# First layer's input products of ten d_ff tiles as blocks of seven products for eight, in passes of batch pairs

## The chip, the cores and the metric

One core of one Trainium2 chip runs the whole program. The metric is device time in microseconds, the median of several runs. Weights arrive as float64 words and are decoded on the chip; every product is made of three fp32r matmuls (high by high, high by low, low by high).

## The reference

```python
x = attention(rmsnorm(q), rmsnorm(k), v)     # 4 batches, 12 heads, 448 rows, 64 wide
x = x.transpose(0, 2, 1, 3).reshape(1792, 768)
h = x @ w_in                                 # first layer, d_ff 2048: 16 tiles of 128
x = np.maximum(h, 0.0) ** 2 @ w_out
g, val = x @ w_gate, x @ w_val               # second layer, d_ff 1536: 12 tiles of 128
out = (g * sigmoid(g) * val) @ w_out2
```

## The kernel before, in words

Everything is kept transposed: a tile is 128 features by 448 rows of one batch, six such tiles are one batch of x. A product of one d_ff tile with one batch is 6 x 3 = 18 matmuls of 128x128 by 128x448 (`in_product`, `mm3`, L370), and so is that tile's share of the output.

**Attention** comes first. Between its matmuls a low-ranked thread (`fillers`, L1056) runs the first layer's d_ff tiles 0 to 5 for batches 0, 1 and 2 (`h_a`, `ya`), and at the end the first three products of batch 3 (`h_lead`, `lead`).

**First layer, rest.** `products` (L1205) walks over `sweeps`: batch 3 with tiles 0 to 10, then the other batches with tiles 6 to 10 and 11 to 15. For each tile: input product `h`, its square on ScalarE and VectorE (`squares`, L405 to L411), and the output product `y` two tiles later. Six PSUM banks collect a sweep's outputs. At its end VectorE adds the partial sum of earlier sweeps, loaded from HBM (`partial_sums`, `written`, L1274), and SyncE's queue stores it. The weights of tiles 6 to 15 are decoded as they come (`load_weights`), x is loaded and split into high and low halves per sweep (`load_x`).

**Second layer.** Gate and value products are taken by Strassen's scheme in Winograd's form, seven block products for eight, for pairs of batches: the operands are halves of the weights (a11, a12, a21, a22 and the sums s1 to s4) and halves of the two batches' x (b11, b21, b22 and the sums t1 to t4). Of each the plain form is stored in HBM, loaded again into a staging tile, and split from there into its final slot (`split_part`, L1452; `load_pair`, L1574). `unit` (L1633) takes the seven products of 9 matmuls each; VectorE adds them up out of PSUM (`plus`, L1677). A pass is three units of one pair of batches, then its twelve output tiles (`outputs`, `summed_out`), each of which VectorE adds to the partial sum loaded from HBM (L1804).

**Order.** The order of every engine's instructions is fixed when the program is built: threads yield jobs with a cost for each engine, and a planner (`dispatch`, `simulate`) gives each engine the best-ranked job that is ready by its own clock. It counts DMAs at 300 bytes per ns (`DMA_RATE`). On the chip the engines follow those lists and wait on semaphores.

Of the kernel before, what the change touches and what calls it, by code (L numbers as in the profile page):

```python
# [9 lines left out]
F32 = mybir.dt.float32  # L10
# [9 lines left out]
KD = DM // 128  # L20
# [5 lines left out]
M1 = 11  # L26
# [20 lines left out]
RAWS2 = 1  # L47
IO_TILES = 7
W2_SLOTS = 16
X_SLOTS = 12  # L50
P_SLOTS = 3
PAIRS = ((2, 0), (1, 3))
GROUP = 3
PARTIALS = 4
SPARES = 2
DEC_AHEAD = 2
PAIR_AHEAD = 3
LEND_RAWS = 0
LEND_TEMPS = 0
SUMS_AHEAD = 4  # L60
SUMS = 4
X_LOADS = 4
OLD_SECOND = 0
BEHIND = 2
X_AT = 3
X_FLIGHT = 3
# [23 lines left out]
PARTS = ("a11", "s2", "a12", "s1", "s4", "s3", "a22", "o0", "o1")  # L90
# [3 lines left out]
def attention_two_ffn_kernel(  # L94
# [27 lines left out]
    x2_d = [[dram.tile([128, S], F32, name=f"x2d{b}_{j}") for j in range(KD)] for b in range(B)]  # L122
    y1_d = [[dram.tile([128, S], F32, name=f"y1d{b}_{j}") for j in range(KD)] for b in range(B)]
    y2_d = [[dram.tile([128, S], F32, name=f"y2d{b}_{j}") for j in range(KD)] for b in range(B)]
    pre_d = [{n: dram.tile([128, WC], F32, name=f"{n}_d{f}") for n in PARTS} for f in range(FF2)]
    t_d = [{n: [dram.tile([128, S], F32, name=f"{n}_d{p}_{k}") for k in range(3)] for n in ("t1", "t2", "t3", "t4")} for p in range(2)]
# [87 lines left out]
    def ported(job, e):  # L214
        return e == "G" or e == "V" and "W" in job[1][0]
# [7 lines left out]
    def dispatch(e):  # L223
# [24 lines left out]
        if e == "S":  # L248
# [51 lines left out]
    wt, placed, free, seen, after = {}, {}, [], set(), []  # L300

    def load_weights(items):
# [7 lines left out]
        def chunk(key, place, c, raw_at):  # L310
# [31 lines left out]
            if c == 0:  # L342
                yield lambda: place or free
                pool, hi_tag, lo_tag = placed[key] = place or free.pop(0)
# [15 lines left out]
        for key, place, rank in items:  # L360
            if not place and after:
                yield lambda: free
                place = free.pop(0)
# [727 lines left out]
    M1B, F1C = range(G1, M1), range(M1, FF1)  # L1091
# [3 lines left out]
    sweeps += [(1, LAST - 1, range(G1, FF1), M1B, y1_d[LAST - 1], x2_d[LAST - 1])]  # L1095
    sweeps += [(1, b, F1C, (), y1_d[b], x2_d[b]) for b in range(LAST - 1)]
    sweeps += [(1, LAST, F1C, F1C, y1_d[LAST], x2_d[LAST])]
    outs = [[out[bass.ts(j, 128), bass.ts(b, S)] for j in range(KD)] for b in range(B)]
    POST = 10000
    when, steps = {}, 0  # L1100
    for layer, b, fs, *_ in sweeps:
        for f in fs:
            for key in (("in", f), ("out", f)):
                when.setdefault(key, POST + steps)
            steps += 1
# [11 lines left out]

    items = [(("in", f), place(4 * f), DEC_FIRST + DEC_STEP * f) for f in range(G1)]
    items += [(("out", f), place(4 * f + 2), OUT_FIRST + OUT_STEP * f) for f in range(G1)]
    later = [(w, f) for f in range(G1, FF1) for w in ("in", "out")]  # L1120
    items += [(key, None, when[key] - W_AHEAD) for key in later]
# [18 lines left out]
    spawn(load_weights(items), 0)  # L1140
    spawn(fillers(), 1e6, FILL)
# [4 lines left out]
    after.append(0)  # L1146
    att.close()
    xp2 = ctx.enter_context(tc.tile_pool(name="xp2", bufs=1, side="right", reuse_waits="tile"))
    mid = ExitStack()
    w2 = mid.enter_context(tc.tile_pool(name="w2", bufs=1, side="right", reuse_waits="tile"))  # L1150
    w3 = mid.enter_context(tc.tile_pool(name="w3", bufs=1, side="right", reuse_waits="tile"))
    raws += [(w3, f"raw{2 + i}") for i in range(RAWS2)]
    was += [(w3, "wa2")]
    wts += [(w3, "wt2")]
    for i in range(W2_SLOTS // 2):
        free.append((w2, f"w{2 * i}", f"w{2 * i + 1}"))
    simulate(lambda: filled and local[FILL] == 0)


    fill.close()  # L1160
    ranked.append(0)
    io = ctx.enter_context(tc.tile_pool(name="io", bufs=1, reuse_waits="tile"))
    io_free = [(io, f"io{i}") for i in range(IO_TILES)]
    ps_y = ctx.enter_context(tc.tile_pool(name="ps_y", bufs=1, space=PSUM, reuse_waits="tile"))

    def x_tiles(n, second, ts):
        def tile_of(j):
            pool = xp2 if second and j < 4 else xp
            ts[j] = pool.tile([128, 2, S], F32R, tag=f"x{j + 2 if second and j >= 4 else j}", name=f"x_{n}_{j}")
            return ts[j]  # L1170

        return tile_of

    def load_x(src, n, tiles, done, rank):

        def part(j, where):
            raw = tile_at(where, [128, S], F32, f"xr_{n}_{j}")
            yield from dma(lambda e: e.dma_start(out=raw, in_=src[j]), 128 * S * 4)
            t = tiles(j)
            yield {"A": 467, "W": 300}, lambda e: copy(e, t[:, 0, :], raw)  # L1180
            yield {"W": 535, "G": 1106}, lambda e: e.tensor_tensor(
                out=t[:, 1, :], in0=raw, in1=as_f32(t[:, 0, :]), op=ALU.subtract
            )
            io_free.append(where)
            done.append(j)

        for j in range(KD):
            yield lambda: io_free and j - len(done) < X_FLIGHT
            spawn(part(j, io_free.pop(0)), rank)

    w_free, x_free, retired = [], [], []

    def release(key):
        del wt[key]
        slot = placed.pop(key)
        if len(seen) < len(items):
            free.append(slot)
        elif slot[0] is w1:
            w_free.extend((w1, tag) for tag in slot[1:])
        else:  # L1200
            retired.append(slot)

    finished = []

    def products():  # L1205
        behind = []
        ys = {}
        xs = x1[LAST]
        k = POST
        for i, (layer, b, fs, last_use, partial, dst) in enumerate(sweeps):  # L1210
            n = f"{layer}_{i}"
            done = None
            for f in fs:
                if f == fs[X_AT if len(fs) > 6 else 1] and i + 1 < len(sweeps):
                    nxt, done = {}, []
                    spawn(load_x(x1_d[sweeps[i + 1][1]], n, x_tiles(n, i % 2 == 0, nxt), done, k), k)
                name = f"{n}_{f}"
                if i == 0 and f < 3:
                    release(("in", f))
                else:  # L1220
                    yield lambda: ("in", f) in wt
                    ps, where = yield from h_tile(f"h_{name}")
                    yield from in_product(ps, wt["in", f], xs)
                    spawn(squares(ps, where, name), k - 0)
                    if f in last_use:
                        release(("in", f))
                while len(behind) >= BEHIND:
                    yield from behind.pop(0)
                sums = {} if partial and f == fs[-1] else None
                if sums is not None:  # L1230
                    spawn(partial_sums(partial, n, sums, k - SUMS_AHEAD), k - SUMS_AHEAD)
                behind.append(out_of(name, n, f, f == fs[0], f == fs[-1], f in last_use, ys, sums, dst, k))
                k += 1
            if done is not None:
                yield lambda: len(done) == KD
                xs = nxt
            if i == len(sweeps) - 2:
                x_free.extend([(xp2, f"x{j}") for j in range(4)] + [(xp, "x6"), (xp, "x7")])
            if i == len(sweeps) - PAIR_AHEAD:
                spawn(load_first_pair(0), k)  # L1240
        x_free.extend((xp, f"x{j}") for j in range(3))
        s_free.extend((xp, f"x{j}") for j in range(3, 6))
        for gen in behind:
            yield from gen
        spawn(spares(), k - W_AHEAD)
        if not OLD_SECOND:
            spawn(pair_sums(1 - passes[0][0], k), k)
        yield from second_layer(k)
        finished.append(0)

    def spares():
        for _ in range(SPARES):
            yield lambda: io_free
            ea_free.append(io_free.pop(0))

    def partial_sums(src, n, sums, rank):

        def part(j, at):
            y = tile_at(at, [128, S], F32, f"yp_{n}_{j}")
# [663 lines left out]
```

## Time and profile before

| | before |
|---|---|
| median of 3 runs | 1231.98 us (1229.92 to 1233.0) |
| the profiled execution | 1228.38 us |
| its span, first to last instruction | 1226.6 us |
| TensorE matmuls | 6426, busy 1205.8 us |
| VectorE busy | 870.6 us |
| ScalarE busy | 630.8 us |
| GpSimd busy | 164.4 us |
| moved by DMA | 238.98 MB |

The span is what the views measure; the execution takes 1.8 us more around it, and the median run 3.6 us more than the profiled one. PE is TensorE, DVE VectorE, ACT ScalarE, POOL GpSimd, SP SyncE. Matmuls overlap in the records, so their pace is read from the length of a piece of the chain over its count, not from the mean of one. The attention's stage ends at 409.67 us, the first layer's at 738.05 us.

### The profile page before, as it was taken

Reading aid. Unit: us, or ns where it says so; the run is one execution under the profiler, and the core shown is the slowest. Engines: PE = TensorE matmul, PEld = TensorE weight load, DVE = VectorE, ACT = ScalarE, POOL = GpSimd, SP = SyncE. Lnnn points to the kernel's source line nnn. Section 1 sums busy time; section 2 is a strip of 40 time slices with the busy share of each in tenths; the row PEclk is TensorE's granted clock in tenths of the full one; section 3 lists DMA queues with packets and bytes.
Section 4 is the critical chain, followed back from the end, with each engine's and each line's share of the span. In section 5 each row is a group of like instructions: output and inputs, shape, how many; then the busy total and the mean of one; then the engine's idle time right before and its main releaser. Section 6 shows DMA issues by size and latency. Waiting matters only on the chain.

```text
span 1226.6 us, 19513 instructions
## 1 busy us (share of the span) xinstructions
PE 1205.8 (98%) x6426; PEld 1032.5 (84%) x6426; DVE 870.6 (71%) x1795; ACT 630.8 (51%) x1381; POOL 164.4 (13%) x280
## 2 busy tenths in 40 slices
PE   8989999999999999999999999999999999999998
PEld 5656667777777899999999999999999999999998
DVE  8999985665543899767665877876678676855564
ACT  6999877766765666333332443564334233422320
POOL 5454464244311000000000000000000000000000
PEclk9999999999999999999999999999999999999999
DMA  7576665334212666878576888876578756752634
GB/s 225 169 206 187 189 186 164 97 127 145 84 41 74 205 195 209 290 248 287 177 261 208 278 264 270 270 242 214 180 237 264 246 185 201 242 183 70 211 120 142
DMA packets 146934, 238.98 MB, mean 195 GB/s; under 512 B 23105, under 2 KB 126418, under 8 KB 146834
## 3 DMA queue, kind: packets, MB, share of 16 engines
q1 hardware_dynamic: 146834, 237.75, 61.0%
q8 instruction: 50, 0.82, 0.3%
q14 instruction: 50, 0.41, 0.1%
HBM read 169.51 MB, written 68.17 MB: 194 GB/s over the span
## 4 chain that ended last, share of the span: by engine, by line
PE 86%; DVE 6%; ACT 4%; DMA 3%; issue 1%; SPq 0%; ACTq 0%; DVEq 0%
PE y L370 28%; PE p L370 23%; PE h L370 13%; PE ya L370 5%; PE o L937 4%; PE h_a L370 4%; PE sc L766 4%; PE pt L897 3%; ACT ring L808 1%; DVE sc L794 1%; ACT turned_p L258 1%; PE pt L892 1%; PE pt L895 1%; PE h_lead L370 1%; DMA raw_out<-in_w_out_dram 1%
## 5 line engine op out<-in xcount | busy, mean ns | idle before, releaser
L370 PE MATMUL y<-s,o_split 128*128 128x448 f32 x864 | 176.7, 365 | 0.0
L370 PEld LDWEIGHTS y<-s,o_split 128*128 128x128 f32 x864 | 162.2, 188 | 13.2 <-DVE s L1321 0.4
L370 PE MATMUL y<-s,hi_out 128*128 128x448 f32 x552 | 157.2, 366 | 1.6 <-DVE r L407 1.6
L370 PE MATMUL h<-x,hi_in 128*128 128x448 f32 x516 | 147.3, 367 | 0.0
L370 PE MATMUL p<-t,s_split 128*128 128x448 f32 x648 | 144.5, 367 | 0.0
L370 PEld LDWEIGHTS p<-t,s_split 128*128 128x128 f32 x648 | 121.8, 188 | 11.1
L808 ACT ACTIVATE ring<-sc,m,rms 128x448 f32<-128x448 f32 x168 | 123.9, 744 | 12.6 <-DVE m L795 4.6
L1677 DVE TENSOR_TENSOR u<-p,u 128x448 f32<-128x448 f32 x144 | 88.3, 621 | 37.5 <-PE p L370 36.1
L370 PEld LDWEIGHTS y<-s,hi_out 128*128 128x128 f32 x552 | 103.5, 188 | 10.5 <-DVE r L407 2.0
L794 DVE TENSOR_REDUCE sc<-sc 128x2 f32<-128x896 f32 (+1 forms) x96 | 93.8, 977 | 16.2 <-PE sc L766 14.8
L370 PEld LDWEIGHTS h<-x,hi_in 128*128 128x128 f32 x516 | 96.9, 188 | 8.4
L370 PE MATMUL y<-s,lo_out 128*128 128x448 f32 x276 | 100.7, 365 | 0.0
L258 ACT COPY turned_p<-pt 128x384 f32<-128x384 f32 (+2 forms) x167 | 88.4, 540 | 23.4 <-PE pt L897 22.6
L370 PE MATMUL p<-b,a_split 128*128 128x448 f32 x432 | 96.2, 367 | 0.0
L370 PE MATMUL h<-x,lo_in 128*128 128x448 f32 x258 | 94.4, 366 | 0.0
L370 PEld LDWEIGHTS p<-b,a_split 128*128 128x128 f32 x432 | 81.1, 188 | 7.1
L937 PE MATMUL o<-turned_p,v 128*64 128x448 f32 x384 | 79.5, 546 | 0.6 <-DVE turned_p L260 0.5
L897 PE MATMUL pt<-ident,ring 128*128 128x128 f32 x432 | 70.7, 274 | 2.8 <-ACT ring L808 2.3
L1804 DVE TENSOR_TENSOR yp<-y,yp 128x448 f32<-128x448 f32 x72 | 43.9, 623 | 38.3 <-PE y L370 21.4
L370 PE MATMUL h_a<-x,hi_in 128*128 128x448 f32 x216 | 67.8, 381 | 0.0
L370 PE MATMUL ya<-sa,hi_out 128*128 128x448 f32 x216 | 67.3, 385 | 0.0
L405 ACT ACTIVATE r<-h 128x448 f32<-128x448 f32 x43 | 23.3, 542 | 81.2 <-PE h L370 81.1
(174 smaller groups left out, 2249.1 us busy)
## 6 DMA issues: line engine op xcount, KB each, us to landing
yp<-y2d SPq DMA_DIRECT2D x72, 224.0 KB
raw_in<-in_w_in_dram SPq DMA_DIRECT2D x32, 384.0 KB
raw_out<-in_w_out_dram SPq DMA_DIRECT2D x32, 384.0 KB
kq<-in_kq_p_dram SPq DMA_DIRECT2D x23, 480.0 KB
t_plain<-t_d SPq DMA_DIRECT2D x48, 224.0 KB
y2d<-yp SPq DMA_DIRECT2D x48, 224.0 KB
raw_a<-in_w_val_dram SPq DMA_DIRECT2D x24, 384.0 KB
raw_a<-in_w_gate_dram SPq DMA_DIRECT2D x24, 384.0 KB
```

Of the source, the lines that this page charges most:

```text
L258: e.copy(out, src)
L370: return {"P": 203}, lambda e: e.matmul(ps, lhsT=w, rhs=x, start=first, stop=last), 0
L405: yield {"A": 424}, lambda e: e.activation(out=r, in_=ps, func=ACTF.Relu)
L766: e.matmul(parts[t][:, :S], lhsT=q[a][d, bass.ts(i % 4, 128)], rhs=k[c][d], start=(p == 0), stop=(p == len(passes) - 1),)
L794: e.tensor_reduce(out=top, in_=sc, axis=AX.X, op=ALU.max, negate=True)
L808: yield {"A": 704}, lambda e: e.activation(out=slot(i), in_=parts[t][:, :S], func=ACTF.Exp, bias=m[:, t:t + 1], scale=rq[:, i:i + 1], accu ...
L892: e.transpose(pieces[:, :, j], p[:, bass.ts(j, 128)] if j < 3 else ends, ident)
L895: e.transpose(ps[:, :128], ends, ident)
L897: e.transpose(ps[:, bass.ts(j + (i > 3), 128)], p[:, bass.ts(j, 128)], ident)
L937: e.matmul(o[64 * h:64 * h + 64], lhsT=v[:, 4 * h + j], rhs=turned_p[:, 4 * h + j if j < 3 else 3], start=(j == 0), stop=(j == 3),)
L1677: return {"V": 535}, lambda e: e.tensor_tensor(out=out, in0=ps, in1=b, op=ALU.add)
L1804: yield {"V": 535}, lambda e: e.tensor_tensor(out=y, in0=ps, in1=y, op=ALU.add)
```

## The change

Tiles 0 to 5 stay as they were. Tiles 6 to 15 become five units of two d_ff tiles: a unit's weights form a 2x2 block matrix (two tiles by two halves of the model dimension), two batches' x the other, and the second layer's `unit` now serves both layers. The first layer becomes six passes: units 0 and 1 for batch pair 0 (batches 0, 1), then for pair 1 (batches 2, 3); unit 2 for pair 1, then pair 0; units 3 and 4 for pair 0, then pair 1. A pass ends with twelve output tiles, each a chain over its units' tiles.

Four more things move with it. Weights of the five units are decoded, summed and stored during attention (`decode_ahead`). Operands are loaded straight into their final slot and split in place (`split_in_place`), with no staging tile; 21 x slots hold one pair's operands. Partial sums of all passes but a pair's last are added into HBM by an accumulating DMA that GpSimd issues, where VectorE added them before. And the last first-layer outputs are handed from SBUF to the sums of the second layer's operands (`handed`).

```diff
+GROUPS1 = ((0, 1), (2,), (3, 4))
...
-    sweeps = [(1, LAST, range(M1), range(G1), None, y1_d[LAST])]
-    sweeps += [(1, b, M1B, (), y1_d[b], y1_d[b]) for b in range(LAST - 1)]
...
+    for layer, groups in ((1, GROUPS1), (2, GROUPS2)):
+        p = 0
+        for us in groups:
+            passes += [(layer, p, us), (layer, 1 - p, us)]
+            p = 1 - p
...
+        f = G1 + 2 * u
+        return [(f"a{r + 1}{c + 1}", w_in[f + r], c) for r in range(2) for c in range(2)], [
...
+    spawn(decode_ahead(), POST)
...
+    def split_in_place(t, src, c):
+
+        plain = as_f32(t[:, 1])
+        yield from dma(lambda e: e.dma_start(out=plain, in_=src), 4 * c * 128)
+        yield from halves_of(t, plain, c)
...
+        for p, a, x, then in (
+            ("p1", "a11", "b11", first_0), ("p6", "s2", "t2", sum_2), ("p2", "a12", "b21", first_0_ends),
+            ("p5", "s1", "t1", sum_4), ("p3", "s4", "b22", first_1), ("p7", "s3", "t3", second_1),
+            ("p4", "a22", "t4", second_0),
+        ):
...
+    def squared(t, at, name):
+
+        yield {"A": 467}, lambda e: e.activation(out=t, in_=t, func=ACTF.Relu)
+        yield lambda: s_free
+        s_at = s_free.pop(0)
+        s = tile_at(s_at, [128, 2, S], F32R, "s_%d_%d_%d_%d" % name)
+        yield {"A": 467}, lambda e: e.activation(out=s[:, 0], in_=t, func=ACTF.Square)
+        yield {"W": 535, "G": 1106}, lambda e: e.tensor_tensor(out=t, in0=t, in1=t, op=ALU.mult)
+        yield {"W": 535, "G": 1106}, lambda e: e.tensor_tensor(
+            out=s[:, 1], in0=t, in1=as_f32(s[:, 0]), op=ALU.subtract
+        )
...
-        if sums is not None:
+        if whole(n):
             yield lambda: (j, h) in sums
...
+            dst = y_of[layer][b][j]
+            yield lambda: (layer, b, j) in y_count
+            yield {"G": POOL_DMA}, lambda e: e.dma_start(out=dst, in_=y, accum_op=ALU.add), 2 * 128 * S * 4, POOL_LATER, True
```

**TensorE, where the first layer's tiles 6 and on begin.** Before, in the sweep of batch 3 (y are outputs, h input products of tile 10, x a k tile's halves):

```order
L370 MATMUL y_1_0_0_5486<-s_1_0_7_5891,hi_out7_5463 128x448 x2
L370 MATMUL y_1_0_0_5486<-s_1_0_7_5891,lo_out7_5464 128x448
L370 MATMUL y_1_0_1_5491<-s_1_0_7_5891,hi_out7_5463 128x448 x2
L370 MATMUL y_1_0_1_5491<-s_1_0_7_5891,lo_out7_5464 128x448
L370 MATMUL h_1_0_10_6094<-x1_18_4511,hi_in10_5758 128x448 x2
L370 MATMUL h_1_0_10_6094<-x1_18_4511,lo_in10_5759 128x448
L370 MATMUL h_1_0_10_6094<-x1_19_4676,hi_in10_5758 128x448 x2
```

And now, behind the outputs of tile 5 (p1 and p6 are block products of pass 0, unit 0):

```order
L370 MATMUL y_1_5903<-s_1_0_5_6121,hi_out5_2679 128x448 x2
L370 MATMUL y_1_5903<-s_1_0_5_6121,lo_out5_2680 128x448
L370 MATMUL p1_0_0_6228<-b11_0_0_5726,a11_1_0_split_5856 128x448 x3
L370 MATMUL p1_0_0_6228<-b11_0_1_5829,a11_1_0_split_5856 128x448 x3
L370 MATMUL p1_0_0_6228<-b11_0_2_5879,a11_1_0_split_5856 128x448 x3
L370 MATMUL p6_0_0_6250<-t2_0_0_5773,s2_1_0_split_5857 128x448 x3
L370 MATMUL p6_0_0_6250<-t2_0_1_5929,s2_1_0_split_5857 128x448 x3
```

An 18-matmul product per tile and batch has become a 9-matmul product, seven of them for two tiles and two batches: 630 in place of 720.

**SyncE's queue, where pass 1 gets its x operands.** Before there was no such load in the first layer; in the second they read (a staging tile, written ahead of the split):

```order
L1586 DMA b11_5_2_plain_11544<-x2d1_2_89 128x448
L1586 DMA t2_5_0_plain_11558<-t2_d1_0_276 128x448
L1586 DMA t2_5_1_plain_11582<-t2_d1_1_277 128x448
L1586 DMA t2_5_2_plain_11599<-t2_d1_2_278 128x448
L1586 DMA b21_5_0_plain_11631<-x2d1_3_90 128x448
```

And now (t2_d and the like are sums stored to HBM; t2_1_2 is the tile of pass 1, into its own slot):

```order
L1321 DMA t3_1_1_6484<-t3_d1_1_1_311 128x448
L1350 DMA t2_d1_1_2_309<-b22_1_1_2_6504 128x448
L1350 DMA t4_d1_1_2_315<-b21_1_1_2_6521 128x448
L1321 DMA t4_1_0_6498<-t4_d1_1_0_313 128x448
L1321 DMA t4_1_1_6522<-t4_d1_1_1_314 128x448
L1321 DMA t1_1_2_6590<-t1_d1_1_2_306 128x448
L1321 DMA t3_1_2_6609<-t3_d1_1_2_312 128x448
L1321 DMA t2_1_2_6628<-t2_d1_1_2_309 128x448
L1321 DMA t4_1_2_6635<-t4_d1_1_2_315 128x448
```

The last sums go out to HBM and come back by the same queue, as the last loads of the pass.

**GpSimd's queue, at the end of pass 0** (yw are output tiles, y1d the partial sums in HBM; there was nothing at this place before):

```order
L1774 DMA y1d1_4_91<-yw_0_4_1_6712 128x448
L1774 DMA y1d0_4_85<-yw_0_4_0_6731 128x448
L1774 DMA y1d1_5_92<-yw_0_5_1_6751 128x448
L1774 DMA y1d0_5_86<-yw_0_5_0_6770 128x448
L1138 TENSOR_TENSOR o2_1_2_split_6896<-o2_1_2_split_6896 128x384
L1138 TENSOR_TENSOR o1_1_2_split_6917<-o1_1_2_split_6917 128x384
```

Twelve accumulating DMAs now stand in GpSimd's list at the end of a pass, with operand splits of the next unit behind them.

## Rows read from the trace of the kernel before

**Rows 1.** The page: busy time by engine, and the chain that ended last.

```profile
PE 1205.8 (98%) x6426; PEld 1032.5 (84%) x6426; DVE 870.6 (71%) x1795; ACT 630.8 (51%) x1381; POOL 164.4 (13%) x280
...
PE 86%; DVE 6%; ACT 4%; DMA 3%; issue 1%; SPq 0%; ACTq 0%; DVEq 0%
```

**Rows 2.** Stretches: length; busy of PE, PEld, DVE, ACT, POOL; clock, DMA share, GB/s.

```profile
180.00:240.00 60.00, 59.45 (x359) 44.53 (x356) 36.27 (x77) 40.77 (x102) 24.41 (x44) 1.00 0.42 132
240.00:300.00 60.00, 60.00 (x364) 44.51 (x364) 35.61 (x80) 40.59 (x101) 23.86 (x43) 1.00 0.43 135
300.00:360.00 60.00, 60.00 (x366) 46.32 (x363) 32.60 (x72) 43.40 (x107) 16.64 (x16) 1.00 0.25 74
420.00:480.00 60.00, 60.00 (x297) 55.30 (x296) 59.94 (x137) 38.78 (x81) 0.00 (x0) 1.00 0.66 208
553.00:581.00 28.00, 28.00 (x139) 25.65 (x138) 20.36 (x42) 9.03 (x18) 0.00 (x0) 1.00 0.85 284
...
443.00:737.80 294.80, 294.80 (x1448) 271.60 (x1447) 219.01 (x449) 123.83 (x245) 4.45 (x4) 1.00 0.74 244
```

**Rows 3.** PE's timeline where attention ends: start, length, what, [idle before].

```profile
409.67 0.57 PE L370 MATMUL y<-s,hi_out 128*128 128x448 f32 x2
410.08 0.37 PE L370 MATMUL y<-s,lo_out 128*128 128x448 f32 x1
412.04 0.47 PE L370 MATMUL y<-s,hi_out 128*128 128x448 f32 x1 [1.59 <-DVE r L407]
```

**Rows 4.** All waits of PE from 400 us to the end.

```profile
PE y L370 <- DVE r L407: 1.6, 1, 1.6
```

**Rows 5.** The chain that ended last: start, length, what.

```profile
455.56 3.68 PE y L370 x18
...
657.60 3.69 PE h L370 x18
...
738.05 11.09 PE p L370 x54
...
859.55 38.71 PE p L370 x189
898.26 21.89 PE y L370 x108
```

**Rows 6.** DVE's timeline in the first layer: start, length, what.

```profile
430.02 0.57 DVE L338 SCALAR_TENSOR_TENSOR wt_out<-wa_out,wt_out 128x384 int32<-128x384 int32 x1
430.50 0.57 DVE L354 TENSOR_TENSOR lo_in<-wt_in,hi_in 128x384 fp32r<-128x384 f32 x1
430.96 0.64 DVE L1181 TENSOR_TENSOR x<-xr,x 128x448 fp32r<-128x448 f32 x1
431.50 0.57 DVE L354 TENSOR_TENSOR lo_out<-wt_out,hi_out 128x384 fp32r<-128x384 f32 x1
431.97 0.38 DVE L331 TENSOR_SCALAR wt_in<-raw_in 128x384 int32<-128x384 uint32 x1
```

**Rows 7.** Groups by line and shape: busy us, mean ns | idle before, releasers.

```profile
L1810 ACT COPY yw<-y 128x448 f32<-128x448 f32 x24 | 12.6, 536 | 13.0 <-PE y L370 10.9 <-DMA a_d<-a 1.3 <-DVE t L1321 0.2
...
L1363 DVE TENSOR_SCALAR a<-raw_a 128x384 int32<-128x384 uint32 x48 | 16.7, 355 | 11.2 <-DMA raw_a<-in_w_gate_dram 8.0 <-DMA raw_a<-in_w_val_dram 3.3
...
L983 POOL TENSOR_TENSOR x<-ox,x 128x448 fp32r<-128x448 f32 x24 | 27.6, 1151 | 70.9 <-ACT x L258 58.9 <-DMA v<-in_v_p_dram 5.9 <-DVE kq L704 2.7
```

**Rows 8.** The chain again: its two longest DMA pieces, issue to landing.

```profile
765.17 4.95 DMA b_plain<-x2d
...
774.37 5.15 DMA raw_a<-in_w_gate_dram
```

**Rows 9.** DMA from 500 to 700 us, in 40 slices of 5 us.

```profile
DMA  6899699469797996867454286978816639989968
GB/s 236 261 342 323 214 318 311 181 147 308 282 320 265 285 360 238 281 179 237 166 171 106 98 268 199 364 292 284 256 68 206 241 130 269 317 236 341 369 210 265
```

More of the change, by code (lines that the diff above doesn't have):

```diff
@@ L25 @@
 G1 = 6
-M1 = 11
 EPS_RMS = 1e-6
@@ L1157, in attention_two_ffn_kernel @@
[L1157 to L1189, printed above, removed]
@@ L1193, in release @@
+    operand, pair_x, summed_x = {}, {}, set()
     def release(key):
         del wt[key]
[L1195 to L1229, printed above, removed]
-                if sums is not None:
[L1231 to L1259, printed above, removed]
-            yield from dma(lambda e: e.dma_start(out=y, in_=src[j]), 128 * S * 4)
-            sums[j] = y, at
-        for m, j in enumerate(OUT_ORDER):
-            yield lambda: io_free and m < sums.get("used", 0) + SUMS
-            spawn(part(j, io_free.pop(0)), rank)
@@ new lines, in attention_two_ffn_kernel, with products @@
+    simulate(lambda: filled and local[FILL] == 0)
+    fill.close()
+    ranked.append(0)
+    given_back.append(0)
+    for at in [at for at in io_free if at in loaned]:
+        io_free.remove(at)
+        x_free.append(at)
+    io = ctx.enter_context(tc.tile_pool(name="io", bufs=1, reuse_waits="tile"))
+    io_free += [(io, f"io{i + 1}") for i in range(IO_TILES)]
+    ps_y = ctx.enter_context(tc.tile_pool(name="ps_y", bufs=1, space=PSUM, reuse_waits="tile"))
+    finished = []
+    def products():
+        k = POST
+        xs = x1[LAST]
+        behind, ys = [], {}
+        for f in range(G1):
+            name = f"1_0_{f}"
+            if f < 3:
+                release(("in", f))
+            else:
+                ps, where = yield from h_tile(f"h_{name}")
+                yield from in_product(ps, wt["in", f], xs)
+                spawn(squares(ps, where, name), k - 2)
+                release(("in", f))
+            while len(behind) >= BEHIND:
+                yield from behind.pop(0)
+            behind.append(first_out(name, f, ys, k))
+            k += 1
+        for j in range(6):
+            s_free.append((xp, f"x{j}"))
+        for gen in behind:
+            yield from gen
+        io_free.extend(ea_free)
+        yield from all_passes()
+        finished.append(0)
@@ new lines, in first_out @@
+    def first_out(name, f, ys, k):
+        yield lambda: ("out", f) in wt and name in ready
+        w = wt["out", f]
+        s, where = ready.pop(name)
+        for j in OUT_ORDER:
+            if f == 0:
+                ys[j] = ps_y.tile([128, S], F32, tag=f"y{j}", name=f"y_{j}")
+            yield from mm3(ys[j], w[0], w[1], bass.ts(j, 128), s[:, 0, :], s[:, 1, :], f == 0, f == G1 - 1)
+            if f == G1 - 1:
+                spawn(first_written(ys[j], j), k - 2)
+        s_free.append(where)
+        release(("out", f))
@@ new lines, in first_written @@
+    def first_written(ps, j):
+        yield settle["P"]
+        yield lambda: io_free
+        at = io_free.pop(0)
+        y = tile_at(at, [128, S], F32, f"ys_{j}")
+        yield {"A": 424}, lambda e: e.copy(y, ps)
+        h_free.append((ps_y, f"y{j}"))
+        yield from dma(lambda e: e.dma_start(out=y1_d[LAST][j], in_=y), 128 * S * 4)
+        y_count[1, LAST, j] = 1
+        io_back(at)
+    y_of = {1: y1_d, 2: y2_d}
+    y_count = {(1, b, j): 1 for b in range(LAST) for j in range(KD)}
@@ L1622, in second_layer, with s_free_w @@
                         spawn(partials(n, p, sums, k), k)
-                yield from unit(n, f, x_of, last_x and f == fs[-1], last_w, k)
+                yield from unit(n, (layer, u), x_of, last_x and u == us[-1], last_w, k)
                 k += 2
-            yield from outputs(n, p, fs, sums if p in summed_before else None, last_w, k)
-            summed_before.add(p)
+            yield from outputs(n, sums, last_w, k)
+    ENDS_1 = 2 * len(GROUPS1)
+    def s_free_w():
+        for _ in range(S_TO_W):
+            spawn(one_s_to_w(), POST)
@@ L1792, in outputs @@
+            yield from chain(j, h, deep[-1:] if m < ahead else deep)
+            spawn(summed_out(n, j, h, ys[j, h], sums), k)
+            if m == last_use[j // 3] and drop_w:
+                for u, r in deep:
+                    w_free.append(operand.pop(((layer, u), f"o{2 * r + j // 3}"))[1])
+        for u, r in deep:
             for h in range(2):
-                s_free.append(ready.pop((n, f, h))[1])
-    def summed_out(n, p, j, h, bank, sums):
+                s_free.append(ready.pop((n, u, r, h))[1])
@@ L1796, in summed_out @@
+    def summed_out(n, j, h, bank, sums):
         ps, where = bank
+        layer, p, _ = passes[n]
         b = PAIRS[p][h]
-        last = all(q != p for q, _ in passes[n + 1:])
-        dst = outs[b][j] if last else y2_d[b][j]
         yield settle["P"]
-        if sums is not None:
+        if whole(n):
             yield lambda: (j, h) in sums
```

754 lines of the change are left out of this document (344 added, 410 removed).

## The prediction

> **What bounds the kernel now.** I read the page first, then the stretches, then TensorE's own timeline and waits. The page shows TensorE busy for 1205.8 us of a span of 1226.6, and its work makes 86% of the chain that ended last [rows 1]; VectorE stands at 71%, ScalarE at 51%. The stretches say the same of the stage that changes: from 443 to 737.8 us TensorE is busy without a gap at a granted clock of 1.00, with VectorE at 219 of 294.8 us and DMA at 0.74 [rows 2]. From 400 us to the end TensorE waits once, 1.59 us at 412 us, for VectorE's square of a tile that is needed at once [rows 3, 4]. So a matmul taken out of this stage shortens the program by its whole length, as long as what feeds TensorE keeps up with a shorter stage.
>
> **The change part by part.**
>
> *Matmuls removed.* The pace is read from pieces of the chain [rows 5]: 18 outputs in 3.68 us, 18 input products in 3.69, 189 block products in 38.71 (0.2048 each), 108 outputs in 21.89 (0.2027). The first layer's stage runs from 409.67 [rows 3] to 738.05 [rows 5]. It holds 774 input-product matmuls (54 of tiles 3 to 5, 720 of tiles 6 to 15) and 828 output matmuls: (328.38 - 1.59) / 1602 = 0.204 us. The change takes seven products of 9 for what were eight, so 720 become 10 x 63 = 630; outputs stay 828, attention's own matmuls and fillers too. 90 x 0.204 = **-18.4 us**, all on the path.
>
> *Pace of what is left.* Blocks and long output chains take 0.2027 to 0.2048 us where they stand now, the stage's mean is 0.204. If the 720 outputs of the passes, now chains over up to four tiles in one bank, ran at 0.2027 for 0.2043, that is -1.2; if not, 0. The block products give nothing. I take -0.3.
>
> *Decoding moved into attention.* Five units' weights are read, decoded, summed and stored there: 139 more VectorE rows before the first first-layer square, 40 raw loads, 40 loads back and the stores between. By the rows of decoding (0.27 to 0.57 us [rows 6]) that is some 57 us of VectorE work. In 180 to 360 us VectorE is busy 36.3, 35.6 and 32.6 of each 60 us and DMA moves 132, 135 and 74 GB/s while TensorE is full [rows 2]: 75 us free on VectorE alone, so I cost it at nothing. Without that cover it would cost up to 57 us; the same work is taken off 420 to 480 us, where VectorE was busy 59.94 of 60 us [rows 2].
>
> *More sums.* Each unit needs seven additions out of PSUM in place of ScalarE's and VectorE's squares straight from it, 70 in all, against 48 partial-sum additions that go; ScalarE gets 96 copies of outputs at 0.54 us [rows 7]. A short pass (one unit, 27.5 us of TensorE) asks VectorE for some 15 rows of the unit (8.0 us), 18 x splits (9.6) and 8 weight splits (3.8), 21.4 us. ScalarE and VectorE are covered by TensorE: nothing. In the stretch 420 to 480 a VectorE busy to 59.94 us still held nobody up [rows 2, 4], so near-full is no stall.
>
> *Start of the first unit.* Before p1 TensorE has 54 input and 108 output matmuls left, 33 us from 409.7. VectorE's list shows 67 rows up to the last operand that unit needs first, about 0.5 us each [rows 6], so 33 us from about 402; the sum operands p5 to p4 follow with some 15 us in hand. Nothing.
>
> *Split in place.* A slot can be loaded only after TensorE's last read of it. The shortest time from freeing to need is pass 2 to 3: 54 block and 72 output matmuls, 25.7 us; elsewhere 33 to 42. One landing in a busy stretch is 4.95 to 5.15 us [rows 8], the cast and the split half a microsecond each [rows 6]: 6.2 us. Hidden.
>
> *Handover of passes.* Here the lists are tight in one place at least. For pass 1 the t2 sum of the third k tile is stored and read back as the last loads on SyncE's queue, then split on VectorE directly ahead of the sum of p6, and cast on ScalarE behind the last output of pass 0. Such a wait isn't in the trace; the nearest row is the 1.59 us at 412, a tile needed at once [rows 3, 4], and one more landing is 5.15 [rows 8]. Bounds 0 to 5.15; I take **+1.6**, because the queue's order leaves the tile behind by a step, not by a whole transfer.
>
> *Accumulating DMAs.* 96 in all: 48 in the first four passes, where they replace a load, a VectorE addition and a store, and 48 in the second layer's. No row of before shows one on GpSimd or its rate. By bytes, SyncE's queue now asks for 76.3 MB from attention's end to the last first-layer load, and 48 accumulates of 0.229 MB count c times: 87, 98, 109 MB for c of 1, 2, 3. Five-microsecond slices reach 369 GB/s where the stage's mean is 244 [rows 9, 2], so 328 us could hold 121 MB; a stretch at 284 GB/s had DMA at 0.85 and TensorE still full [rows 2]. Taken at nothing for c of 2; they begin to cost, on the mean, at c of 3.9. For the issue itself the nearest GpSimd row is a tensor operation of 1.15 us [rows 7]: twelve take 13.8 us of a 27.5 us pass. Nothing. In the second layer the same DMAs and splits in place have passes of three units (189 block and 108 output matmuls, 38.71 + 21.89 us [rows 5]), over twice the time: nothing there either. The Trainium skill's page "SBUF — State Buffer" ("A bandwidth-pool intuition that's wrong") speaks against this: a DMA from GpSimd that takes about 620 ns alone took about 3100 ns beside a VectorE copy, since its descriptors wait for a shared port. By that figure twelve would need 37 us of a 27.5 us pass and the sum would be 19 us higher, an estimate from that page that no run here bears out yet; VectorE's rows are short here (0.355 us [rows 7] to 0.64 [rows 6]).
>
> *Sum.* -18.4 - 0.3 + 1.6 = -17.1. The profiled execution took 1228.38, so 1211.3; the median of the runs shown is 3.6 higher, 1231.98, so 1214.9: **1215 us**.
>
> **The rivals.** A measurement of this kernel can tell about 0.3% from no change, 3.7 us: "same" is 1228.3 to 1235.7.
>
> *1. DMA becomes the bound at the handovers.* From pass 0 to 1 the list has 33 loads and stores (7.6 MB) and 12 accumulates in 54 + 144 + 15 matmuls, 43.3 us, which hold 16.0 MB at 369 GB/s [rows 9]: enough up to c of 3.05. From 2 to 3 it is 5.8 MB and 12 accumulates in 38.4 us: again 3.05. At c of 4, or as much lost to small transfers, each is 7.1 us late, 14.2 in all: 1229. For it: the stage's mean was already 0.74 busy, the slices swing between 68 and 369 [rows 9], and the planner counts 300 bytes per ns with no landing delay. Against: TensorE never waited at 0.85 [rows 2, 4]. The Trainium skill's "DMA: Bandwidth & Descriptors" (Issuing engines are not separate DMA queues) holds that GpSimd's transfers share the same engines, so that its queue brings no bandwidth of its own; the runs here show nothing on that yet. 1222 to 1229, chance 0.17 (0.11 of it faster, 0.06 same).
>
> *2. GpSimd's queue becomes the bound, and the kernel slower.* Each output tile lies in a buffer until its accumulating DMA is through, the buffers stop ScalarE's copies, these the PSUM banks, these TensorE. With T us for each DMA on GpSimd, passes 2 and 3 (27.5 us, twelve each) decide from T = 2.3; the loss is 2 x (12 T - 27.5). Slower by over 0.3% needs T above 3.15; T = 3.5 gives 1215 + 29 = 1244. For it: nothing in the trace prices such a DMA, and split operands stand behind them in GpSimd's list. Against: the nearest GpSimd row, 1.15 us [rows 7]. Chance 0.11 (0.10 slower). The page named above would give T = 3.1 and 1234, just inside "same" (0.01).
>
> **How the numbers follow.** The forecast has 0.72. Its own range is 1210 (no handover wait, the full -1.2 of pace, and some 2 us for the draw of a median whose runs lie 3.1 apart) to 1219 (a wait of 5.15). With rival 1 at its upper end the range becomes 1210 to 1229; outside lie rival 2 and what of the forecast falls below. Faster 0.72 + 0.11 = 0.83; same 0.06 + 0.01 = 0.07; slower 0.10.
>
> **What would show it.** In the profile after, TensorE's count should be 6336, the first layer should end at about 721 us with the second unchanged in length, and attention should end within 2 us of 409.67. Waits of TensorE, if any, should stand at p6 of pass 1 and sum to under 5 us. GpSimd's DMAs should lie under 2.3 us apart, no slice of the first layer should stay at 369 GB/s for 15 us, and VectorE should gain load in 180 to 360 and lose it in 420 to 480. Rival 1 would show waits at each first product of a pass, released by DMA; rival 2 waits of outputs behind ScalarE's copies, those behind GpSimd. I am wrong in the main if attention's end moves or if waits exceed 7 us; wrong in the pace if 189 block products of the first layer take other than 38.7 us.

## The result, and the profile after

The change made the kernel slower: 1242.59 us (1240.6 to 1244.87, four runs) against 1230.95 for the kernel before in the same session, a ratio of 1.0093 with a 95% interval of 1.0070 to 1.0117. The forecast was 1215, the range 1210 to 1229, and "slower" had a chance of 0.10.

| | before | after |
|---|---|---|
| median | 1230.95 us | 1242.59 us |
| span of the profiled execution | 1226.6 | 1240.7 |
| first outputs behind attention's last wait | 412.04 [rows 3] | 431.89 (+19.85) |
| from there to the second layer's first product | 326.01 (to 738.05 [rows 5]) | 314.57 (-11.44) |
| from there to the end of the span | 488.55 | 494.24 (+5.7) |

The three differences add up to the 14.1 us between the two spans. 412.04 stands behind three outputs that had already run and 431.89 ahead of them, so like for like attention moved by 0.6 us more, and the first layer gained 0.6 us more. The first layer did get shorter. What ate its gain stands ahead of it, in attention, and to a smaller part behind it.

The page of the changed kernel, busy time and the chain that ended last, against [rows 1]:

```profile
PE 1199.1 (97%) x6336; PEld 1017.5 (82%) x6336; DVE 919.5 (74%) x1877; ACT 705.0 (57%) x1550; POOL 289.9 (23%) x411
...
PE 69%; DVE 10%; DMA 9%; ACT 7%; issue 3%; SPq 1%; POOL 0%; DVEq 0%; ACTq 0%; POOLq 0%
```

The 90 matmuls are gone (6426 to 6336), but TensorE's share of the chain fell from 86% to 69%, and VectorE, ScalarE and DMA share what it lost: the end is now set in part by chains that run through them. The stretches say where, with the columns of [rows 2]:

```profile
180.00:240.00 60.00, 54.85 (x327) 39.18 (x324) 42.54 (x93) 38.36 (x94) 23.39 (x39) 1.00 0.68 209
240.00:300.00 60.00, 58.25 (x347) 43.21 (x347) 48.89 (x107) 47.23 (x115) 24.45 (x38) 1.00 0.71 211
300.00:360.00 60.00, 55.49 (x322) 40.71 (x322) 43.26 (x99) 42.92 (x106) 20.00 (x29) 0.97 0.63 189
```

TensorE was full here before; now it lacks 1.8 to 5.2 us in each 60, while VectorE never passes 49 and ScalarE 48 of 60. So no engine is the bound by its load: something is late. Two views of waits in attention name it. TensorE's two longest, the second of them the one that ends attention (without it, its waits from 180 us on come to 12.0 us):

```profile
PE pt L897 <- DVE ox L959: 4.6, 3, 2.7
PE y L370 <- DVE r L407: 4.4, 1, 4.4
```

and ScalarE's for the raw words of weights, which the change decodes here (total, times, longest):

```profile
ACT raw_o L1163 <- DMA raw_o<-in_w_out_dram: 22.4, 11, 6.4
...
ACT raw_a L1163 <- DMA raw_a<-in_w_in_dram: 12.0, 7, 3.9
```

ScalarE stood still for 34 us in these two groups, waiting for words, with attention's rows behind it in its fixed list (in the kernel before, its waits for words of weights came to 7.5 us in the same stretch). One such place, on all engines' timelines:

```profile
338.58 0.98 SPq L1160 DMA_DIRECT2D raw_a<-in_w_in_dram  x2
...
343.46 0.58 ACT L1163 ACTIVATE raw_a<-raw_a 128x384 f32<-128x384 f32 x1 [3.90 <-DMA raw_a<-in_w_in_dram]
...
343.46 0.36 DVE L1169 TENSOR_SCALAR raw_a<-raw_a 128x384 int32<-128x384 uint32 x1 [2.93 <-DMA raw_a<-in_w_in_dram]
...
346.68 0.61 DVE L959 TENSOR_TENSOR ox<-o,zb 128x448 f32<-128x448 f32 x1
...
347.35 0.90 PE L897 MATMUL pt<-ident,ring 128*128 128x128 f32 x3 [2.67 <-DVE ox L959]
```

Read it from the top: two loads of raw words are issued at 338.6; ScalarE and VectorE both reach the rows that read the first of them and stand until 343.46, 4.9 us after its issue. With nothing ahead of it the planner counts 1100 + 393216 / 300 + 900 ns, 3.3 us, for such a load. Behind the decoding stands `ox`, the quotient that attention's next transpose waits for, and TensorE idles 2.67 us. Then something follows that the waits don't show; stretches with their granted clock:

```profile
347.30:350.50 3.20, 3.15 (x10) 2.90 (x11) 2.55 (x5) 3.17 (x9) 3.17 (x3) 0.50 0.72 186
...
432.60:435.80 3.20, 3.20 (x10) 2.80 (x10) 2.56 (x6) 0.75 (x2) 0.00 (x0) 0.50 0.99 322
```

After an idle time of 2.67 us, and again after one of 4.39 us at 431.89, TensorE was granted 0.50, the lower of its levels (1.2 GHz), for over 3 us. The 4.39 us are not a wait for a load: VectorE is busy throughout, for the most part with sums and splits of the passes' x that its list has ahead of the square.

```profile
427.50:431.80 4.30, 0.00 (x0) 0.00 (x0) 4.30 (x9) 2.77 (x6) 0.37 (x1) 1.00 0.49 120
```

Of the 19.85 us, the 12.0 us of waits, the last wait's 2.8 us over the 1.59 of before and the first fall of the clock (1.8, if it cost what the second did) make up 16 to 17; the rest shows as no wait of TensorE. The price of a fall is in the chain, whose rows answer to [rows 5]:

```profile
431.89 5.47 PE y L370 x18
...
441.00 3.64 PE y L370 x18
...
466.54 25.92 PE p L370 x126
492.46 29.18 PE y L370 x144
...
583.87 4.54 DMA t<-t_d
591.16 1.24 DVE u L1690
592.99 12.82 PE y L370 x62
...
746.46 38.89 PE p L370 x189
...
841.64 4.38 DMA raw_a<-in_w_val_dram
853.22 16.48 PE y L370 x80
```

The same 18 outputs take 5.47 us at the lower clock and 3.64 later: 1.8 us. In the passes, block products run at 25.92 / 126 = 0.2057 us and outputs at 29.18 / 144 = 0.2026. Where the chain leaves TensorE, it goes over an operand's load, or over raw words of the second layer's weights, to a square or a gate that the outputs need. All waits of TensorE from 440 us on:

```profile
PE y L370 <- DVE s L1691: 3.2, 4, 1.3
PE y L370 <- DVE s L1138: 2.6, 3, 1.1
```

They are 5.8 us in all, 3.2 in the first layer and 2.6 in the second, all at outputs and none at a pass's first product. Without these waits and the 1.8 us of clock the first layer's stage of the changed kernel would be 17.0 us shorter than before, like for like, against 18.7 forecast without its wait.

### The profile page after: what moved, and what is told of

Its sections match the earlier page's. It is cut to its first block, busy times and chain, and to the rows that moved or that the text cites. A ratio compares the mean times of both kernels' runs of the same rounds, so it can differ in the third digit from the quotient of the medians.

```text
span 1240.7 us, 20299 instructions
## 1 busy us (share of the span) xinstructions
PE 1199.1 (97%) x6336; PEld 1017.5 (82%) x6336; DVE 919.5 (74%) x1877; ACT 705.0 (57%) x1550; POOL 289.9 (23%) x411
## 3 DMA queue, kind: packets, MB, share of 16 engines
q1 hardware_dynamic: 155762, 248.37, 63.4%
q0 software_dynamic: 13824, 22.03, 10.9%
## 4 chain that ended last, share of the span: by engine, by line
PE 69%; DVE 10%; DMA 9%; ACT 7%; issue 3%; SPq 1%; POOL 0%; DVEq 0%; ACTq 0%; POOLq 0%
PE p L370 32%; PE y L370 26%; ACT ring L808 3%; DMA raw_a<-in_w_in_dram 2%; PE ya L370 2%; PE o L937 2%; PE h_a L370 2%; PE sc L766 2%; DMA raw_o<-in_w_out_dram 2%; DVE sc L794 2%; ACT turned_p L262 1%; PE pt L897 1%; DMA a_d<-a 1%; PE h L370 1%; DMA nat<-in_k_n_dram 1%
## 5 line engine op out<-in xcount | busy, mean ns | idle before, releaser
L370 PE MATMUL y<-s,o_split 128*128 128x448 f32 x1584 | 326.2, 366 | 6.0 <-DVE s L1691 3.2
L370 PEld LDWEIGHTS y<-s,o_split 128*128 128x128 f32 x1584 | 296.8, 188 | 33.2 <-DVE s L1138 4.7
L370 PE MATMUL p<-t,s_split 128*128 128x448 f32 x918 | 205.4, 368 | 0.0
L370 PEld LDWEIGHTS p<-t,s_split 128*128 128x128 f32 x918 | 172.5, 188 | 16.2
L1759 ACT COPY yw<-y 128x448 f32<-128x448 f32 x120 | 63.3, 535 | 77.2 <-PE y L370 68.7
L897 PEld LDWEIGHTS pt<-ident,ring 128*128 128x128 f32 x432 | 52.0, 141 | 20.8 <-DVE ox L959 6.8
L370 PE MATMUL p<-t,a_split 128*128 128x448 f32 x306 | 68.8, 369 | 0.0
L370 PE MATMUL p<-b,s_split 128*128 128x448 f32 x306 | 68.3, 367 | 0.0
L370 PEld LDWEIGHTS p<-t,a_split 128*128 128x128 f32 x306 | 57.5, 188 | 5.7
L370 PEld LDWEIGHTS p<-b,s_split 128*128 128x128 f32 x306 | 57.5, 188 | 5.6
```

Source lines behind the costliest of these rows:

```text
L370: return {"P": 203}, lambda e: e.matmul(ps, lhsT=w, rhs=x, start=first, stop=last), 0
L897: e.transpose(ps[:, bass.ts(j + (i > 3), 128)], p[:, bass.ts(j, 128)], ident)
L1759: yield {"A": 424}, lambda e: e.copy(y, ps)
```

## The experiments

Theory 1: ScalarE and VectorE stand in their fixed order behind raw words that land later than the planner assumes, and attention stands behind them. Theory 2: the added work itself delays attention. Theory 3: the added traffic makes attention's own transfers land late. "Start" is the first output behind attention's last wait, 412.04 before and 431.89 after.

**Rows placed later behind their load** (`raw_3us_later`), work and traffic the same:

```diff
         yield from dma(lambda e: e.dma_start(out=raw, in_=src[:, bass.ts(c, WC), :]), 8 * WC * 128)
+        if not ranked:
+            yield RAW_LATER
         high, low = raw[:, :, 1], raw[:, :, 0]
```

RAW_LATER is 3000 ns; `not ranked` is attention and the little behind it.

> The changed kernel, but the planner waits 3 us longer after each load of raw weight words during attention before it places the rows that read them; same work, other places in the lists. Theory 1 (ScalarE and VectorE stand in their fixed order behind raw words that land later than the list assumes, and attention's rows stand behind them): the first layer's outputs behind attention start at 414 to 422 us in place of 431.9, TensorE's waits in attention fall from 12 us to under 6, ScalarE's waits for raw words from 38 us to under 15, time 1230 to 1237. Theory 2 (the added VectorE and ScalarE work itself delays attention): start at 429 to 434, time within 3 us of 1242.6. Theory 3 (the added traffic makes attention's own transfers land late): the same as theory 2.

Start 420.69, ScalarE's waits for raw words 4.3 us; TensorE's own waits in attention came to 7.0 us, over the 6 expected, and the time stayed: 1241.77 us, ratio 1.0085 (1.0052 to 1.0119). ScalarE's waits in attention, the start, and TensorE's longest wait in the passes:

```profile
ACT raw_o L1166 <- DMA raw_o<-in_w_out_dram: 2.8, 1, 2.8
ACT raw_a L1166 <- DMA raw_a<-in_w_in_dram: 1.5, 1, 1.5
```

```profile
420.69 0.67 PE L371 MATMUL y<-s,hi_out 128*128 128x448 f32 x2 [2.21 <-DVE r L408]
```

```profile
PE y L371 <- DVE yp L1756: 6.9, 1, 6.9
```

Eleven microseconds of attention came back by placing alone, as theory 1 has it, and the total missed its 1230 to 1237. Each of the two raw buffers was now held 3 us longer, so decoding ran on into the passes: 37 loads of raw words had been issued by the start, where the change had issued 44, and ScalarE waits 19.7 us for `raw_o` between 440 and 760 us. The 6.9 us fall at the end of the last first-layer pass. There the addition of a partial sum stands on VectorE behind splits of the next pass's operands, whose x (`b<-y1d`) was still being loaded from 728.9 to 734.4. That late decoding pushed them there is a reading; it is tried below with a third buffer.

**No raw loads** (`no_raw_loads`): only the first load into each raw buffer stays, and the decoding rows run on what the buffers hold. The trace has 2 loads where the change has 112, so 110 are left out (38 of the first layer's units, 72 of the second's), not the 62 of 64 of the expectation.

```diff
+        if raw_at in raw_of:
+            raw = raw_of[raw_at]
+            yield 3300
+        else:
+            raw = raw_of[raw_at] = raw_at[0].tile([128, WC, 2], I32, tag=raw_at[1], name=f"raw_{name}")
+            yield from dma(...)
```

> The changed kernel without 62 of its 64 loads of raw weight words for the block products of both layers: the decoding rows run all the same, on what the two raw buffers hold, so the weights are not decoded and the output is another. Theory 1: start behind attention at 412 to 418 us, and the waits for s in the passes (5.8 us in all, and the longer output stages of 23.7 for 22.05 us in the second layer) go too; time 1215 to 1224. Theory 2: start still at 428 to 432, time 1232 to 1240. Theory 3: start at 412 to 420 as by theory 1, but the run beside it (the old kernel with more moves) tells the two apart.

One run, 1221.59 us, and the start at 416.21:

```profile
416.21 0.67 PE L370 MATMUL y<-s,hi_out 128*128 128x448 f32 x2 [1.92 <-DVE r L407]
```

All VectorE rows of the decoding were there, and attention was 4.2 us longer than before instead of 19.9 (1.8 of the 4.2 were lost by 164 us, after a fall of the granted clock at 41.6). Theory 2 falls as the main cause. Waits after 440 us came to 2.7 us in place of 5.8, so loads of raw words stood behind about half of those too.

**More traffic in the kernel before** (`before_more_moves`):

```diff
+    def one_move(m):
+        src = w_tiles["in"][m % FF1].bitcast(I32)[:, bass.ts(m // FF1 % 2, 768)]
+        t = dram.tile([128, 768], I32, name=f"more{m}")
+        yield from dma(lambda e: e.dma_start(out=t, in_=src), 4 * 768 * 128)
```

> The kernel before with 64 more DMAs of 393 KB each (25.2 MB) from 178 us on, every 3.3 us, from the weights to scratch in HBM, which nobody reads. Theory 3: attention's end moves by 10 us or more (first outputs behind it at 422 or later in place of 412.0), time 1241 or more. Theories 1 and 2: at most 3 us, start at 412 to 415, time 1230 to 1235.

One run, 1234.25 us; a stretch of attention, with as much traffic as the changed kernel or more, and the start (the planner counts the added moves too, so from there on its lists are not those of before):

```profile
240.00:300.00 60.00, 60.00 (x363) 45.68 (x364) 34.09 (x81) 43.38 (x109) 24.50 (x37) 1.00 0.79 256
```

```profile
415.20 0.68 PE L370 MATMUL y<-s,hi_out 128*128 128x448 f32 x2 [2.20 <-DVE r L407]
```

TensorE stays full with DMA at 0.79 and 256 GB/s. The start is 3.2 us later, but most of that is older than the traffic. The same 16 matmuls of attention, first before and then here, and a stretch here:

```profile
161.10 3.23 PE L937 MATMUL o<-turned_p,v 128*64 128x448 f32 x16
```

```profile
164.48 3.23 PE L937 MATMUL o<-turned_p,v 128*64 128x448 f32 x16
79.20:86.00 6.80, 6.61 (x25) 3.37 (x27) 6.36 (x17) 6.09 (x18) 2.08 (x2) 0.50 0.59 172
```

This execution was 3.4 us behind at 164 us, after falls of the granted clock to 0.50 at 41.7 and 79.2, and the first added move was issued at 180.1. At attention's last 16 such matmuls (392.62 before, 396.40 here) it was 3.8 us behind. So the traffic is worth well under 1 us here, and theory 3 falls too.

**No accumulating DMAs** (`no_accum`): in every pass with an earlier part, the partial sum is loaded, added by VectorE and stored by SyncE.

```diff
-        if whole(n):
+        if before_it(n):
             yield lambda: (j, h) in sums
...
-            yield {"G": POOL_DMA}, lambda e: e.dma_start(out=dst, in_=y, accum_op=ALU.add), 2 * 128 * S * 4, POOL_LATER, True
+            yield from dma(lambda e: e.dma_start(out=y_of[layer][b][j], in_=y), 128 * S * 4)
```

> The changed kernel with its partial sums loaded, added by VectorE and stored by SyncE in every pass, and no accumulating DMA on GpSimd. If the accumulating DMAs (7 us to land, 11.8 at most) hold buffers and banks and so cause the waits in the passes: the waits for s after 440 us fall from 5.8 us to under 2, output stages come to 22.1 us, time 1232 to 1237. If these waits come from VectorE and ScalarE standing behind late loads: the waits stay at 4 us or more, the start behind attention stays at 430 to 433, and the time is 1241 to 1248, since VectorE gets 84 additions more and the queue 84 loads.

1239.86 us, ratio 1.0075 (1.0057 to 1.0094): between the two ranges, and not to be told from the change's 1.0093. The waits for `s` fell to 1.9 us, but a new one came, VectorE's additions standing behind the splits of the next pass's operands:

```profile
PE y L370 <- DVE yp L1757: 4.3, 1, 4.3
```

This alone doesn't settle what the accumulating DMAs are worth. It also shows a spread to keep in mind: its lists for TensorE, ScalarE and VectorE are the change's own up to the end of attention, yet its start is 427.43 where the change's is 431.89. A single profile is good for differences of ten microseconds, not of four.

**A third raw buffer, alone and with later rows** (`third_raw`, `third_raw_3us`, `third_raw_4us_splits`). The buffer lives in attention's pool, for one attention output buffer less:

```diff
-OX_BUFS = 2
+OX_BUFS = 1
+THIRD_TO = 150
...
+                if not third:
+                    third.append((ap, "raw2"))
+                    raws.append(third[0])
...
-        raws.append(raw_at)
+        if raw_at[0] is not ap or expd[0] < THIRD_TO:
+            raws.append(raw_at)
```

The second adds RAW_LATER = 3000 as above. The third has 4000, and in `split_in_place`:

```diff
         yield from dma(lambda e: e.dma_start(out=plain, in_=src), 4 * c * 128)
+        if c == WC:
+            yield SPLIT_LATER
```

with SPLIT_LATER = 2000 ns: weight operands only, in all passes.

> The changed kernel with a third buffer for raw words during attention (an attention output buffer is given up for its space); rows are placed behind loads by the same rule as in the change. Theory 1 (rows stand in line behind words that land later than the list assumes): a buffer alone moves loads and rows forward together, so ScalarE still waits over 25 us for raw words, the outputs behind attention start at 425 to 433 us, time 1238 to 1247. Rival (loads are late because they wait for a free buffer): start at 413 to 421, ScalarE's waits under 15 us, time under 1232.

> The same third buffer, and in attention the rows that read raw words are placed 3 us later than in the change. Theory 1: start at 414 to 421 us as with two buffers (420.7), but decoding is no longer pushed into the passes, so the 6.9 us wait of the sixth pass is gone and the time is 1224 to 1233. If what was given back there came from something else than late decoding (the accumulating DMAs, the order of partial sums): waits after 440 us stay over 10 us and the time stays at 1238 to 1244.

> Third buffer, rows behind raw words 4 us later in attention, and casts of weight operands placed 2 us later behind their loads in all passes. If theory 1 holds for the passes too: start at 414 to 421 us, waits after 440 us under 4 us (7.7 with the wait at the start left out is 5.8 in the change), second layer 486 to 488 us long in place of 490.6, time 1220 to 1228, faster than the kernel before. If the passes' waits come from the accumulating DMAs or the traffic: waits after 440 us at 5 to 8 us, time 1227 to 1234.

The buffer alone: 1242.19 us, ratio 1.0090 (1.0075 to 1.0106), start 427.55, and ScalarE waits longer than in the change:

```profile
ACT raw_o L1164 <- DMA raw_o<-in_w_out_dram: 28.4, 14, 4.4
...
ACT raw_a L1164 <- DMA raw_a<-in_w_val_dram: 8.8, 3, 3.8
ACT raw_a L1164 <- DMA raw_a<-in_w_in_dram: 6.8, 6, 1.9
```

The buffer and 3 us: 1224.90 us, ratio 0.9953 (0.9939 to 0.9967), no wait of ScalarE for a decoding row's words in attention, and start at 416.58:

```profile
416.58 0.68 PE L372 MATMUL y<-s,hi_out 128*128 128x448 f32 x2 [2.10 <-DVE r L409]
```

These two kernels differ in one number, by which their rows stand in another order (and a row that two engines can do may change engine): the same work, buffers and bytes, and 17.3 us. Of the 15.6 us between the two profiled spans 11.0 are there at the start, and 4.6 come behind it. For attention theory 1 is shown. The third version also gives the casts of weight operands 2 us: 1222.61 us (1220.8 to 1225.6, six runs), ratio 0.9938 (0.9922 to 0.9955), the fastest of all. Its start, its waits after 440 us, and its chain:

```profile
420.13 0.67 PE L373 MATMUL y<-s,hi_out 128*128 128x448 f32 x2 [1.83 <-DVE r L410]
```

```profile
PE p L373 <- DVE t L1141: 1.4, 1, 1.4
PE y L373 <- DVE s L1702: 0.9, 1, 0.9
```

```profile
731.00 38.89 PE p L373 x189
769.89 21.89 PE y L373 x108
```

The 1.4 us are in front of the last product of the short pass 3: VectorE's split of a t operand stands behind additions that wait for TensorE. All eight second-layer passes now take these 60.8 us. From the start to the second layer it is 310.87 us, 15.1 less than before; from there to the span's end 489.8, 1.3 more than before.

**Decoding after attention** (`dec_late`), DEC_FROM = 168 in place of 0:

> The changed kernel with its decoding for the block products started only after the last softmax of attention. If attention is longer through the decoding as a whole (theories 1, 2 and 3 alike): start behind attention at 411 to 416 us. If the rest of the change (order, buffers, the pair's operands) moves it: 420 or later. The passes then wait for weights: TensorE waits 30 to 80 us for splits of weight operands, time 1260 to 1310.

One run, 1282.11 us, start 412.43. Attention's whole shift is the decoding's, and the passes then starve: TensorE waits 51 us in them, most of all for casts of x operands and not for the splits of weights that were expected:

```profile
PE p L370 <- ACT t L262: 24.2, 4, 14.8
```

**The best version without accumulating DMAs** (`best_no_accum`), the edit of `no_accum` on `third_raw_4us_splits`:

> The version with the third buffer, rows 4 us later behind raw words and casts of weight operands 2 us later, but partial sums loaded, added by VectorE and stored by SyncE in place of all accumulating DMAs. If the accumulating DMAs cost something in themselves (7 us to land, their traffic): time under 1220, ratio to the kernel before under 0.991, second layer under 485.5 us. If they are free once rows stand behind their loads: second layer 486 to 487 us, the short passes wait 1 to 5 us for partial sums, time 1223 to 1229, ratio 0.994 to 0.999.

1231.11 us (twelve runs), ratio 1.0008 (0.9990 to 1.0026). The time is 2 us above the second expectation's; its mechanism is seen. The second layer's passes stay at 60.8 us, and the loss is in the short passes, where an output waits for VectorE's addition of a partial sum, which stands behind splits of the next pass's operands, and from 589.1 to 595.9 the granted clock is 0.50:

```profile
PE y L373 <- DVE yp L1768: 4.6, 1, 4.6
```

From its first block product to the second layer it needs 286.0 us (451.78 to 737.80), with accumulating DMAs 278.4 (452.62 to 731.00). Once rows stand where their data is, the accumulating DMAs are worth 8.5 us between the medians, 0.7% by the two ratios (the two versions were measured in different sessions, each against the kernel before).

## Why the prediction was wrong

**Decoding moved into attention**, costed at nothing, is the step that failed: it cost 19.85 us. The 75 us that VectorE had free in [rows 2] were there, and no_raw_loads shows that the rows fit into them. But free time in a 60 us mean isn't free time at a place in a list. The change put 40 loads in front of rows of two engines that run their lists in order, and 34 us of waits of ScalarE, with VectorE's beside them, stood ahead of attention's own rows. I counted landings for the operands of the passes and not for the words of the decoding, which come by the same queue, although one of the two rows that I took them from is a load of such words [rows 8].

**Matmuls removed** (-18.4) held. In the version whose rows stand right, 15.1 us are gone from this stage with 2.3 us of waits in it, 17.4 without them, against 18.7 with the term of the pace. **The pace** accounts for part of the rest: outputs took the 0.2026 that was the lower bound, 0.7 us better than taken, but block products 0.2057 where the row of [rows 5] had 0.2048, and 630 x 0.0017 against the stage's mean of 0.204 is 1.1 us back. 0.9 us are left without a name. **The second layer** was forecast unchanged and was 5.7 us longer: 2.6 are waits, 1.4 the block products' pace (38.89 for 38.71 in each of eight passes), the rest lies in the same three output stages. With rows placed later 1.3 us are left, all of them pace.

**Handover of passes** (+1.6, at p6 of pass 1) was mis-sized and misplaced: 5.8 us of waits, none at p6 and all at outputs, about half of them behind loads of raw words by no_raw_loads; with rows placed 4 and 2 us later 2.3 us are left. **The start of the first unit** never held up p1, as forecast, but sums and splits of x stand on VectorE ahead of a square, and TensorE's wait there grew from 1.59 to 4.39 us. **Split in place** held up no block product in the changed kernel, but its loads (`t<-t_d` in the chain above) are among those whose readers kept a square behind them, and in the fastest version one product waited 1.4 us for such a split, in a short pass.

**Accumulating DMAs**: nothing, as said (the bound on the mean comes out at c of 4.1 from the prediction's own numbers, not 3.9, which decided nothing). By the page, their queue takes 10.9% of the engines' time for 22.03 MB where SyncE's takes 63.4% for 248.37:

```profile
q1 hardware_dynamic: 155762, 248.37, 63.4%
q0 software_dynamic: 13824, 22.03, 10.9%
```

That is 0.495 for 0.255 per MB, c = 1.94 where 2 was taken; no row had given that 2, so it was a guess that came out. GpSimd was busy 1.1 and 0.9 us with each, far below the 2.3 from which **rival 2** decides:

```profile
L1774 POOL DMA_DIRECT2D y1d<-yw x48 | 42.2, 1135 | 60.2 <-ACT yw L1759 60.1
L1774 POOL DMA_DIRECT2D y2d<-yw x48 | 41.8, 919 | 92.3 <-ACT yw L1759 86.7 <-DMA s_d<-a 5.2 <-issue 0.2
```

So the kernel became slower, but not by that rival. The Trainium skill's 3100 ns for a DMA from GpSimd beside a VectorE copy ("SBUF — State Buffer", "A bandwidth-pool intuition that's wrong") isn't seen in GpSimd's time here, 1135 and 919 ns; the rows beside it on VectorE are additions and splits for the most part, not copies. **Rival 1** had the kind of loss right (a landing later than the planner counts) and the place and resource wrong: in attention, where most was lost, the DMA engines stood at 0.63 to 0.71 and the rows were simply early. It also had the planner wrong: beside 300 bytes per ns it does count 1100 and 900 ns for each DMA, and that was too little.

What stays open in part is the 8 us by which the best version's attention still ends after 412.04. Its profile shows TensorE's longest wait in attention, 2.44 us, with VectorE's rows ahead of it:

```profile
334.51 0.56 DVE L1146 TENSOR_TENSOR a<-a,a 128x384 f32<-128x384 f32 x1 [2.65 <-DMA a_d<-a]
334.99 0.68 DVE L267 COPY turned_p<-pt 128x512 f32<-128x512 f32 x1
335.77 3.32 PE L940 MATMUL o<-turned_p,v 128*64 128x448 f32 x16 [2.44 <-issue]
```

The view names no releaser, but the matmuls read `turned_p`, whose copy ends at 335.67, behind a sum of weights that stood 2.65 us for its part to come back from HBM. RAW_LATER doesn't cover that load: the same fault, one step on. The execution had also lost 3.2 us by 164 us, after falls of the clock at 40.9 and 81.9; best_no_accum has the same lists up to the start and no such falls, and starts at 419.29, so little of that lasts. The rest may be the order of the lists, and wasn't tried apart.

## What to carry to other kernels

Work that is moved under another stage has to be costed by what its rows wait for, not by the free time of the engine: on an engine that runs in order, a row that waits for a load stops everything behind it, however idle the engine is. Where a planner orders the rows, compare its landing time with one that a trace shows, and give loads the buffers to be late in; one number and one buffer turned a loss of 0.9% into a gain of 0.5%. Look at the waits of the engines that feed the bottleneck before and after, since their totals (34 us here) show the fault before TensorE's (12 us) do. But ask of each wait what stands behind it: in the fastest version ScalarE waits 57 us for raw words after 440 us, and TensorE 2.3.

## What the runs showed of the hardware that was not expected

TensorE's granted clock fell to 0.50 for over 3 us after single idle times of 2.67 and 4.39 us, and stayed at 1.00 behind the 1.59 us of the kernel before; the second fall cost 1.8 us beside the wait itself. The length of one idle time alone doesn't tell which it will be. In third_raw_3us the clock fell after 2.10 us (at 418.1) and after 1.83 us (at 578.5); it stayed at 1.00 after 2.20 us in before_more_moves and after 2.44 us in third_raw_4us_splits:

```profile
578.50:581.90 3.40, 3.40 (x10) 2.97 (x10) 3.40 (x8) 1.85 (x4) 0.00 (x0) 0.50 0.09 29
```

```profile
415.20:418.60 3.40, 3.40 (x16) 3.11 (x17) 3.40 (x9) 1.76 (x4) 0.00 (x0) 1.00 0.51 134
```

An accumulating DMA from GpSimd occupied its engine for about 1 us and the DMA engines for 1.94 times the time per byte of SyncE's transfers.
